# Scan constants in a PSUM bank, scans in two parts, turns in the channel mix's banks: a linear-attention and mixer kernel on one core

## The chip, the core and the metric

The kernel runs on one core of one Trainium2 chip. Its engines work side by side, each through its own list of instructions in order: TensorE (PE, with its weight loads as PEld), VectorE (DVE), ScalarE (ACT), GpSimd (POOL) and SyncE (SP), which issues the DMAs. The metric is the device time of one execution in microseconds, as the median of several runs; lower is better.

## The reference, cut to what matters

Four sequences of 768 steps go through a linear attention with a decay `w` per channel (8 heads of 48 channels), and its output `x` through a mixer: a low-rank mix over the steps (`U`, `V`, rank 32) and a channel mix (384 to 1536 to 384).

```python
for t in range(S):                                   # S = 768, state is [B, H, 48, 48]
    cur = einsum('bhd,bhe->bhde', u * k[t], v[t])
    y[:, :, t] = einsum('bhd,bhde->bhe', r[t], state + cur)
    state = w[t][..., None] * state + einsum('bhd,bhe->bhde', k[t], v[t])
...
h = x.transpose(0, 2, 1) @ U @ V
u = x + h.transpose(0, 2, 1)
return u + maximum(u @ w_ch1, 0.0) @ w_ch2
```

## The kernel before, in words

**Chunks.** Each sequence is cut into 6 chunks of 128 steps, so there are 24 chunks `g`. In a chunk the 8 heads lie as 4 pairs on 128 partitions, channels on partitions, steps along the free dimension. The running products of the decay come from two scans on DVE. `scan_f` (L387) runs backwards over `w` of all four pairs, 517 elements, with the constant `resets`, which is 1 at the border of a pair and 0 elsewhere, and so starts a new product in each pair. `tots` takes each pair's full product; a reciprocal (L423) puts its inverse into the border places of `qd`, which is 0 elsewhere, and `scan_q` (L400) runs forward over 516 elements with `qd`. Both constants lie in SBUF. Then `r` is multiplied with the result `Q` (step RP, L407) and `k` with `F` (step KS, L412), in place in the tile `rk`; each of these products runs on DVE or on GpSimd, as the order says. There is one buffer for `Q` and there are two for `F`.

**The rest of a chunk.** The scores (AM, into `aps`) are matmuls of the scaled `rk`. The diagonal, with the bonus `u`, comes from the products PR and MD in the first six chunks, and from RK, RU and a reduction RED on `kr` in the others; ACT or GpSimd lays it out as `A`; CP copies the scores above it under a mask (L557, L555). YA and YZ make `y`, DS the state's increment, ZA and ZM add and decay it. XE copies `y` into `xT`.

**Turns.** `k` (KT, copied out by ACT in L529) and `x` (XT, copied out in L743) are turned on PE for the first twelve chunks, later on DVE in blocks of 32. On PE these turns, and MD, write one PSUM bank of their own (`tr`, pool `psT`).

**Mixer.** When a sequence's six chunks are there, GA multiplies `x` with `U`: six chunk products of 32 rows and 384 columns, four beside each other, then two that add to the first two (L762). SELM and GSL (L782) make `gs` from it, HP (L816) the mix, UADD, UH and UL the two parts of `u`. The channel mix takes seven blocks of 384 or 512 steps. UP (L865) makes twelve groups of nine matmuls per block, each into one of three PSUM banks (`ffn`), which ACT and DVE empty (HH L870 or L872, HL L876). DN (L899) makes three sums per block, each in four quarters of nine matmuls, emptied by L917. The weights come as raw 64-bit words and are converted piece by piece (C2, C3 on DVE, E and HI on ACT, ADD on GpSimd, the remainder SUB, L339).

**What sets the order.** All steps stand in a list, and the table `ORDER` gives the sequence in which they are issued: three characters a step, its number, whether it goes to its other engine, and how many warming matmuls on constant data (`lead`, L200) go ahead of it. Each engine runs its steps in that sequence and waits by semaphores for what they need. Buffers and banks are handed out in the same sequence.

PSUM has eight banks: two for the scores, one each for the turns, `y` and the state, and three for the channel mix.

Of the kernel before, what the change touches and what calls it, by code (L numbers as in the profile page):

```python
# [20 lines left out]
P = 128  # L21
# [12 lines left out]
SEG = P + 1  # L34
# [17 lines left out]
def channel_order():  # L52
# [25 lines left out]
    "8I18w08y18x02505z08i02I02W02402O08l02K08m06A08n02109606W08o02L05+06G02608z02706X08j06a02c02218p09216Y19G06b0"
    "2802912X02Q09402Y02R02P09312M02N12S06e06f02d09s06H06K09702Z02j06c08u02T02U16L09J08k19L02l02e06g02a06h16d12k0"
    "6M08s02m09B09C09H06Z12f02g02n02q02b16N06l06O09506I02o16m09k06x09D06n02s09O19r09P02h06Q09M02r02i19E06y09Q02t0"  # L80
    "7106z06R07212u09j09K02p19l02v07302w17707806S0BB09F0Bc09N09R19t1BC09n09u19S19T09o09Y09806T0BE0BL09m17909W06U0"
    "6P09U19I09v09V16o09p16p09909X09q09Z09w19A16V0BJ06u06i06q0BR0Bb09a0BK0BG09y09b06J09x1BH0Be0C50BM06j06k09z0Bf1"
    "CY09d0BI1Bg06v06w09e0BN0Bj0BS07A0C806r07B0CF09f07D09+0Bl09c17C06s0Bh09-0Bk0CG1Bi1C916t07E0BV0BO0CH09g0BD0BP1"
    "6+0CA0740BT06-0BQ07F0BU0C607009h0CE0BW0D20Br0750A007G0760CX0A10Bm0CB0CI07H0Ch0D10BF1BZ0A30CD1A20Ca0A40BX0A50"
    "Bv0Bn0Ci1CC1Bo0CL0D407I0A60A70C707J07M0A807K07N07O0Bs0CJ1CK0A907P0Cc0BY1Bd0Cd0Cj0Cg0DT0Ck07S0Bt0AA0Bu0AD07Q0"
    "Dd0AE0AB0Ba07T0CM0AH0Bp0DB0Bq1AF0Bw07U0Bx0CP0AI0AJ0DA0Cf0B+0B-0DC1CN0Ga07V0AC0DU0By0Cn0Ce1CQ0D907W0AK0H40AG0"
    "AL0Gb0Bz17L0De0Gc0D60Co0CO0Ag0AM0AN0Am0D70CZ0An0Cb0GA0Ah0DW0AX0Ao0GQ0Cp0H50Ai0D81D50AU0AR0DD0AY0AZ0Cl1Db0Aa0"
    "C00AV07X0Dc0C10DY0GT07R0Cq0CR0DE0DZ0GR0CS0AW0Cr0Cm1CU0Da1Cs0DH0DV0CV0CT1Ad0Ct0Ab0G10Gd0CW0Cw0AS1AT0DI0Ac0DF1"
    "Cu0GB0C20Cx0Ae0D30GY0Af0DX1DL0AO0Cv1DG1G00DM0Df0Ap0Aj0Dg0DJ0AP0Dh0Cy0DQ0DR0Dj0AQ0DK0DN0Ge1G30Ak0Al0GC0As0Ha0"
# [1133 lines left out]
```

## Time and profile before

| | before |
|---|---|
| median of 3 runs | 450.12 us (448.71 to 450.27) |
| the profiled execution's own time | 448.02 us |
| its span on the core | 446.3 us |
| PE busy | 426.4 us (96%) |
| DVE busy | 362.7 us (81%) |
| ACT busy | 189.7 us (42%) |
| GpSimd busy | 104.0 us (23%) |

The span runs from the first instruction to the end of the last. Busy times are those of engine instructions; matmuls are pipelined and their ends modelled, so a busy PE may still wait a little between matmuls. The shares hide three stretches: up to the first up-projection at 68.3 us, from there to the last token-mix correction at 335.0 us, and the rest, in which only the channel mix is left.

### The profile page before, as it was taken

What the parts mean: (1) busy time and instruction counts of PE and PEld (TensorE: products, weight loads), DVE (VectorE), ACT (ScalarE), POOL (GpSimd) and SP (SyncE); (2) the same over time, 40 slices, a digit from 0 to 9 for tenths busy, and PEclk for the clock granted to TensorE, in tenths of its full rate; (3) what the DMA queues carried; (4) which work ended last, traced back from release to release, by engine and by line L of the source; (5) the groups of instructions that cost most, each with busy time, mean ns of one, the idle gap of its engine ahead of it and who ended that gap; (6) DMA issues with size and microseconds to landing.
All of it is one profiled execution on the core that took longest, in us unless ns stands there. A gap on an engine that the chain in (4) does not pass through costs nothing.

```text
span 446.3 us, 9868 instructions
## 1 busy us (share of the span) xinstructions
PE 426.4 (96%) x3906; PEld 366.1 (82%) x3906; DVE 362.7 (81%) x750; ACT 189.7 (42%) x533; POOL 104.0 (23%) x123
## 2 busy tenths in 40 slices
PE   6996999999999999999999999999999999999993
PEld 4785759999999898788868788887767889999993
DVE  8999999999899999999999999999995116524610
ACT  5697988776476332565023323013634002112300
POOL 1112232432257555332225101420000100100000
PEclk9996799999999999999999999999999999999998
DMA  8966836244654635331307030174212130133020
GB/s 298 337 232 225 271 124 220 87 153 151 223 171 164 220 106 181 107 115 37 107 32 241 3 93 0 46 225 164 74 66 77 36 122 21 59 127 110 1 78 24
DMA packets 23911, 57.22 MB, mean 128 GB/s; under 512 B 2864, under 2 KB 7856, under 8 KB 23856
## 3 DMA queue, kind: packets, MB, share of 16 engines
q1 hardware_dynamic: 23856, 56.50, 38.0%
q8 instruction: 32, 0.52, 0.5%
q14 instruction: 23, 0.19, 0.1%
HBM read 51.77 MB, written 4.72 MB: 127 GB/s over the span
## 4 chain that ended last, share of the span: by engine, by line
PE 40%; DVE 16%; issue 1%; ACT 1%; DVEq 0%
PE f L899 20%; PE f L865 16%; DVE xn L720 5%; DVE kn L685 2%; DVE hid L876 2%; DVE xn L718 1%; DVE A L555 1%; DVE F L387 1%; PE aps L542 1%; DVE Q L400 1%; PE hp L816 1%; DVE xT L917 1%; PE y L622 1%; DVE Z L593 0%; PE y L632 0%
## 5 line engine op out<-in xcount | busy, mean ns | idle before, releaser
L865 PE MATMUL f<-u,w1h 128*128 128x384 f32 (+1 forms) x504 | 147.9, 364 | 1.0 <-DVE hid L876 1.0
L899 PE MATMUL f<-hid,w2h 128*128 128x384 f32 (+1 forms) x504 | 148.3, 364 | 0.0
L865 PEld LDWEIGHTS f<-u,w1h 128*128 128x128 f32 x504 | 92.9, 188 | 12.6 <-DVE hid L876 2.5
L899 PEld LDWEIGHTS f<-hid,w2h 128*128 128x128 f32 x504 | 92.9, 188 | 10.0 <-issue 1.3
L865 PE MATMUL f<-u,w1l 128*128 128x384 f32 (+1 forms) x252 | 90.7, 360 | 0.0
L899 PE MATMUL f<-hid,w2l 128*128 128x384 f32 (+1 forms) x252 | 90.7, 360 | 0.0
L870 ACT ACTIVATE hid<-f 128x384 fp32r<-128x384 f32 (+1 forms) x65 | 34.6, 538 | 106.6 <-PE f L865 104.0
L876 DVE SCALAR_TENSOR_TENSOR hid<-f,hid 128x384 fp32r<-128x384 f32 (+1 forms) x84 | 50.2, 606 | 13.4 <-ACT hid L870 12.5
L454 ACT ACTIVATE A<-ident,dv 128x128 f32<-128x128 f32 x148 | 46.6, 391 | 11.7 <-DVE dv L440 3.9
L899 PEld LDWEIGHTS f<-hid,w2l 128*128 128x128 f32 x252 | 47.4, 188 | 4.7
L865 PEld LDWEIGHTS f<-u,w1l 128*128 128x128 f32 x252 | 47.4, 188 | 4.1
L685 DVE STREAM_TRANSPOSE kn<-rk 32x128 f32<-32x128 f32 x160 | 48.3, 302 | 2.4
L917 DVE TENSOR_TENSOR xT<-f,xT 128x384 f32<-128x384 f32 (+1 forms) x21 | 12.8, 613 | 37.6 <-PE f L899 37.2
L322 POOL TENSOR_TENSOR cva_w<-cva_w,raw_w 128x384 int32<-128x384 int32 x24 | 26.2, 1100 | 70.1 <-DVE cva_w L315 51.9
L832 POOL TENSOR_TENSOR u<-xT,u 128x512 fp32r<-128x512 f32 (+1 forms) x11 | 13.5, 1236 | 92.0 <-DVE u L828 85.1
L387 DVE TENSOR_TENSOR_SCAN F<-w,resets 128x517 f32<-128x517 f32 x24 | 30.6, 1275 | 0.4 <-DMA w<-in_wT 0.2
L720 DVE STREAM_TRANSPOSE xn<-xT 32x192 f32<-32x192 f32 x80 | 29.6, 370 | 1.3 <-ACT xT L666 0.2
L400 DVE TENSOR_TENSOR_SCAN Q<-w,qd 128x516 f32<-128x516 f32 x24 | 29.3, 1223 | 0.1
L407 POOL TENSOR_TENSOR rk<-rk,Q 128x512 f32<-128x512 f32 x12 | 16.4, 1365 | 45.0 <-DVE Q L400 42.3
L461 POOL TENSOR_SCALAR_AFFINE_SELECT A<-dv 128x128 f32<-128x128 f32 (+1 forms) x33 | 11.5, 382 | 58.1 <-PE f L865 23.3
L602 ACT ACTIVATE Z<-Z,tots 128x96 f32<-128x96 f32 x60 | 17.5, 364 | 10.3 <-DVE Z L593 10.2
L1088 ACT ACTIVATE junk<-raw_w 128x384 uint8<-128x384 f32 x24 | 13.1, 544 | 19.7 <-DMA raw_w<-in_w 19.5
(123 smaller groups left out, 570.8 us busy)
## 6 DMA issues: line engine op xcount, KB each, us to landing
raw_w<-in_w SPq DMA_DIRECT2D x48, 384.0 KB, 3.9
rk<-in_rkT SPq DMA_DIRECT2D x24, 512.0 KB, 4.3
kr<-in_rkN SPq DMA_DIRECT2D x18, 384.0 KB, 4.5
w<-in_wT SPq DMA_DIRECT2D x24, 258.5 KB, 2.8
v<-in_vS SPq DMA_DIRECT2D x24, 224.0 KB, 3.9
out_dram<-xT SPq DMA_DIRECT2D x12, 192.0 KB, 2.6
out_dram<-xT SPq DMA_DIRECT2D x9, 256.0 KB, 2.5
raw_V<-in_V SPq DMA_DIRECT2D x8, 96.0 KB, 3.4
```

The lines of the kernel that those rows point to most:

```text
L322: lambda: nc.gpsimd.tensor_tensor(out=d["to"].bitcast(I32), in0=d["a"].bitcast(I32), in1=d["e"], op=ALU.add),
L387: nc.vector.tensor_tensor_scan(out=F[:, ::-1], data0=st["w"][:, ::-1], data1=resets[:, ::-1], initial=1.0, op0=ALU.mult, op1=ALU.add)
L400: nc.vector.tensor_tensor_scan(out=st["Q"], data0=st["w"][:, 0:n], data1=qd, initial=0.0, op0=ALU.mult, op1=ALU.add)
L454: nc.scalar.activation(to, one, AF.Copy, scale=dv[:, NP * i + j : NP * i + j + 1])
L602: nc.scalar.activation(st["Z"][:, j], src[:, j], AF.Copy, scale=nxt[:, j : j + 1])
L685: nc.vector.transpose(a, b)
L720: nc.vector.transpose(to[q, :, :, r], src[r, :, :, q])
L865: nc.tensor.matmul(ps, wt[:, f, ct, :], u[ct][:, z], start=(m == 0), stop=(m == 8))
L870: nc.scalar.activation(h[:, 0], d["ps", f], AF.Relu)
L876: nc.vector.scalar_tensor_tensor(out=h[:, 1], in0=d["ps", f], scalar=0.0, in1=h[:, 0].bitcast(F32), op0=ALU.max, op1=ALU.subtract)
L899: nc.tensor.matmul(d["o", ct], wt[:, 4 * ct + part, f - 3 * part, :], hid[f][:, z], start=(part == 0 and m == 0), stop=(part == 3 and m == 8),
L917: nc.vector.tensor_tensor(out=o, in0=d["o", ct], in1=o, op=ALU.add)
```

## The change

- The two constants of the scans become one, `qd`, in a PSUM bank that nothing else uses (pool `psQ`). The turns' bank is given up for it. A bank holds 512 numbers, so a pair's stretch in `w`, `F` and `Q` becomes 130 long (`SEG`), and each scan runs as two instructions over two pairs each, 259 elements for F and 258 for Q; both halves read overlapping parts of `qd` (shifted by `OVER`). The inverses of the first and third pair go into a small tile `starts`, from which the Q scan takes its start value; those of the second and fourth go into `qd`. So the step R is two reciprocals.
- The turns of `k` and `x` and MD take one of the channel mix's three banks (`ffn`).
- In GA the products of the last two chunks of a sequence are each cut into two of 192 columns, so that four narrow ones stand beside each other and add to the four first sums.
- Small things: `blank`, 256 wide, takes the place of `resets` as data of the warming matmuls, and `w` in memory has the new stretch length.
- `ORDER` is a new table. Over the whole program it moves from DVE to GpSimd 5 products KS, 7 RP, 3 PR, 4 RK, 1 RU and 8 remainders SUB; five high parts HH go from DVE to ACT, three UH and two HI the other way; two decays ZM go from ACT to DVE.

```diff
-SEG = P + 1
+SEG = P + 2
+OVER = NP * SEG - NP * P
...
 ORDER = (
-    "2x03603002y03113203O03712z03303M03513P03V00J03803900L03400K03N03R03W13C03E23S02-03A10003D00200M00Q04e03B13X0"
+    "2x02y02z03M03N03000J03200003603712-03303803V03P03n03R03W13o00L03503903413Q10K03C03U03A14D03D03E03S03113T13X0"
...
-    psT = pool("psT", 1, space=PSUM)
     psY = pool("psY", 1, space=PSUM)
+    psQ = pool("psQ", 1, space=PSUM)
...
-    qd = const.tile([P, NP * SEG], F32, name="qd")
+    qd = psQ.tile([P, NP * P], F32, name="qd")
     nc.vector.memset(qd, 0.0)
+    nc.vector.memset(qd[:, SEG - 1 : NP * P : 2 * SEG - OVER], 1.0)
+    starts = const.tile([P, 2], F32, name="starts")
...
         def scan_f():
-            F = st["F"] = place("F", [P, NP * SEG + 1], f"F_{g}", buf["F"])
-            nc.vector.tensor_tensor_scan(
-                out=F[:, ::-1], data0=st["w"][:, ::-1], data1=resets[:, ::-1], initial=1.0, op0=ALU.mult, op1=ALU.add
-            )
+            F = st["F"] = place("F", [P, n], f"F_{g}", buf["F"])
+            for h in range(2):
+                a, e = 2 * SEG * h, 2 * SEG * (h + 1)
+                back = lambda t, o=0: t[:, a + 1 - o : e - o][:, ::-1]
+                nc.vector.tensor_tensor_scan(
+                    out=back(F), data0=back(st["w"]), data1=back(qd, OVER * h), initial=1.0, op0=ALU.mult, op1=ALU.add
+                )
...
         def scan_q():
             st["Q"] = place("Q", [P, n], f"Q_{g}", buf["Q"])
-            nc.vector.tensor_tensor_scan(
-                out=st["Q"], data0=st["w"][:, 0:n], data1=qd, initial=0.0, op0=ALU.mult, op1=ALU.add
-            )
+            for h in range(2):
+                a, e = 2 * SEG * h, 2 * SEG * (h + 1) - 2
+                nc.vector.tensor_tensor_scan(
+                    out=st["Q"][:, a:e], data0=st["w"][:, a:e], data1=qd[:, a - OVER * h : e - OVER * h],
+                    initial=starts[:, h : h + 1], op0=ALU.mult, op1=ALU.add,
+                )
...
-        rc = step(
-            "R " + nm, "DVE", lambda: nc.vector.reciprocal(qd[:, 0:n:SEG], st["F"][:, 1:n:SEG]), [f],
-            take=[buf["qd"]], use=[buf["F"]],
-        )
+        def invert():
+            tot = segs(st["F"])[:, :, 1]
+            nc.vector.reciprocal(starts, tot[:, 0:NP:2])
+            nc.vector.reciprocal(qd[:, SEG : NP * P : 2 * SEG - OVER], tot[:, 1:NP:2])
+
+        rc = step("R " + nm, "DVE", invert, [f], take=[buf["qd"]], use=[buf["F"]])
...
         def turn_k():
-            tr = st["trk"] = place("tr", [P, NP, P], f"trk_{g}", btr)
+            tr = st["trk"] = place("ffn", [P, NP, P], f"trk_{g}", btr)
...
-            for c in cs:
-                p0 = 32 * (c % 4)
+            n = 4 // len(cs)
+            for m in range(4):
+                c, w = cs[m // n], DM // n
+                cols = slice(m % n * w, m % n * w + w)
+                x = xns[b, c]["xn"].rearrange("p a b -> p (a b)")
                 nc.tensor.matmul(
-                    d["ga"][p0 : p0 + 32, :], U_sb[:, c, :], xns[b, c]["xn"], start=(c < 4), stop=(c >= NCH - 4)
+                    d["ga"][32 * m : 32 * m + 32, cols], U_sb[:, c, :], x[:, cols], start=(n == 1), stop=(n > 1)
                 )
```

What the new table does is seen best on the engines themselves. First DVE at the start of the program, before: the scans of the chunks 0 and 1 (`F`, `Q`), the pair product (`kr`), the products with `F` and `Q` (`rk`), the inverse (`RECIPROCAL`) and the first weight conversions (`cva`). A scan is listed here as SCALAR_TENSOR_TENSOR on L387 or L400 (L393 and L408 in the changed kernel).

```order
L387 SCALAR_TENSOR_TENSOR F_143<-w_140,resets 128x517
L423 RECIPROCAL qd<-F_143 128x4
L486 TENSOR_TENSOR kr_151<-rk_145 128x512
L400 SCALAR_TENSOR_TENSOR Q_154<-w_140,qd 128x516
L412 TENSOR_TENSOR rk_145<-rk_145,F_143 128x512
L387 SCALAR_TENSOR_TENSOR F_159<-w_156,resets 128x517
L302 TENSOR_SCALAR cva_w_1_171<-raw_w_1_162 128x384
L407 TENSOR_TENSOR rk_145<-rk_145,Q_154 128x512
L423 RECIPROCAL qd<-F_159 128x4
```

DVE at the same place, now:

```order
L393 SCALAR_TENSOR_TENSOR F_150<-w_141,qd 128x259 x2
L433 RECIPROCAL starts<-F_150 128x2
L434 RECIPROCAL qd<-F_150 128x2
L497 TENSOR_TENSOR kr_160<-rk_143 128x512
L408 SCALAR_TENSOR_TENSOR Q_164<-w_141,starts,qd 128x258 x2
L393 SCALAR_TENSOR_TENSOR F_173<-w_146,qd 128x259 x2
L433 RECIPROCAL starts<-F_173 128x2
L434 RECIPROCAL qd<-F_173 128x2
```

Each scan and each inverse is two instructions now, and the products of `rk` with `F` and `Q` are gone from here.

GpSimd's first products before are weight conversions alone:

```order
L322 TENSOR_TENSOR cva_w_1_171<-cva_w_1_171,raw_w_1_162 128x384
L322 TENSOR_TENSOR cva_V_300<-cva_V_300,raw_V_265 96x384
L322 TENSOR_TENSOR U_sb<-cva_U_207,raw_U_203 128x192
L322 TENSOR_TENSOR cva_w_2_326<-cva_w_2_326,raw_w_2_210 128x384
L322 TENSOR_TENSOR cva_w_0_482<-cva_w_0_482,raw_w_0_475 128x384
```

GpSimd's first products now:

```order
L421 TENSOR_TENSOR rk_143<-rk_143,F_150 128x512
L416 TENSOR_TENSOR rk_143<-rk_143,Q_164 128x512
L421 TENSOR_TENSOR rk_148<-rk_148,F_173 128x512
L416 TENSOR_TENSOR rk_148<-rk_148,Q_215 128x512
L324 TENSOR_TENSOR cva_w_1_184<-cva_w_1_184,raw_w_1_153 128x384
L497 TENSOR_TENSOR kr_243<-rk_182 128x512
L497 TENSOR_TENSOR kr_247<-rk_203 128x512
L341 TENSOR_TENSOR w1l<-cva_w_1_184,w1h 128x384
L416 TENSOR_TENSOR rk_182<-rk_182,Q_260 128x512
```

The products that left DVE stand here, ahead of the conversions and between them.

PE in the third chunk before: the turns of `k` (`trk`) and `x` (`trx`) share one bank, with other steps between them.

```order
L550 MATMUL aps<-rk_255 128x128 x8
L739 MATMUL trx_1_405<-ident,xT_275 128x128 x3
L564 MATMUL dS<-v_374,kn_324 48x48 x8
L520 MATMUL trk_421<-ident,rk_255 128x128 x4
L622 MATMUL y_452<-A_380,v_374 32x128 x8
```

PE there now:

```order
L561 MATMUL aps<-rk_182 128x128 x8
L575 MATMUL dS<-v_289,kn_308 48x48 x8
L503 MATMUL trd_392<-u_diag,kr_247 128x2 x4
L531 MATMUL trk_401<-ident,rk_182 128x128 x4
L531 MATMUL trk_408<-ident,rk_203 128x128 x4
L633 MATMUL y_433<-A_274,v_289 32x128 x8
```

MD (`trd`) and two turns of `k` stand side by side, in three of the channel mix's banks.

## Rows read from the trace of the kernel before

**Rows 1.** The page: busy us, share of the span and instructions of each engine.

```profile
PE 426.4 (96%) x3906; PEld 366.1 (82%) x3906; DVE 362.7 (81%) x750; ACT 189.7 (42%) x533; POOL 104.0 (23%) x123
```

**Rows 2.** Busy time of each engine by stretch; the first row names the columns.

```profile
core 0: us, PE busy (x) PEld busy (x) DVE busy (x) ACT busy (x) POOL busy (x), PEclk, DMA share, GB/s
0.00:68.30 68.30, 59.44 (x706) 44.81 (x707) 64.78 (x112) 53.00 (x158) 16.05 (x23) 0.90 0.72 244
...
26.00:36.00 10.00, 7.65 (x140) 6.03 (x133) 9.05 (x16) 8.86 (x28) 1.76 (x2) 1.00 0.64 222
36.00:50.00 14.00, 12.16 (x141) 9.64 (x142) 13.78 (x26) 11.19 (x33) 4.86 (x4) 0.51 0.80 265
...
68.30:333.70 265.40, 262.07 (x2645) 223.22 (x2644) 255.79 (x551) 117.80 (x323) 83.64 (x96) 1.00 0.38 124
333.70:446.30 112.60, 104.86 (x559) 98.03 (x558) 42.13 (x89) 18.88 (x55) 4.27 (x4) 0.98 0.20 68
```

**Rows 3.** Two lines' instructions: ns min/median/max, first and last start in us, forms.

```profile
L865 PE MATMUL f<-u,w1h x504: 332/336/505, 68.3 to 419.9; 128*128 128x384 f32 x96, 128*128 128x512 f32 x72
L782 DVE TENSOR_TENSOR gs<-gb,gs x4: 555/555/555, 63.7 to 335.0; 32x384 fp32r<-32x384 f32 x4
```

**Rows 4.** The chain that ended last, in order of time: start us, us, what.

```profile
253.87 2.08 PE f L865 x9
...
396.82 1.56 PE f L865 x9
```

**Rows 5.** The scans' and the inverse's lines, columns as in rows 3.

```profile
L387 DVE TENSOR_TENSOR_SCAN F<-w,resets x24: 1200/1226/2275, 3.6 to 292.4; 128x517 f32<-128x517 f32 x24
L400 DVE TENSOR_TENSOR_SCAN Q<-w,qd x24: 1211/1222/1233, 5.6 to 299.2; 128x516 f32<-128x516 f32 x24
L423 DVE RECIPROCAL qd<-F x24: 154/174/183, 4.9 to 295.1; 128x4 f32<-128x4 f32 x24
```

**Rows 6.** DVE: groups by form (busy us, mean ns), one line, a back-to-back pair.

```profile
L339 DVE TENSOR_TENSOR w1l<-cva_w,w1h 128x384 fp32r<-128x384 f32 x12 | 6.7, 555 | 0.1
L821 DVE TENSOR_TENSOR xT<-hp,xT 128x512 f32<-128x512 f32 x9 | 6.1, 683 | 0.5 <-PE hp L816 0.4
...
L407 DVE TENSOR_TENSOR rk<-rk,Q x12: 662/682/692, 8.7 to 268.7; 128x512 f32<-128x512 f32 x12
...
53.86 1.00 DVE L315 SCALAR_TENSOR_TENSOR cva_w<-raw_w,cva_w 128x384 uint32<-128x384 uint32 x2
L315 DVE SCALAR_TENSOR_TENSOR cva_w<-raw_w,cva_w 128x384 uint32<-128x384 uint32 x24 | 13.2, 556 | 0.1
```

**Rows 7.** Scans beside GpSimd's products: one line, then instructions by time (start, us).

```profile
L407 POOL TENSOR_TENSOR rk<-rk,Q x12: 1181/1202/2043, 84.0 to 300.5; 128x512 f32<-128x512 f32 x12
...
178.58 2.27 DVE L387 TENSOR_TENSOR_SCAN F<-w,resets 128x517 f32<-128x517 f32 x1
178.57 1.20 POOL L407 TENSOR_TENSOR rk<-rk,Q 128x512 f32<-128x512 f32 x1 [2.66 <-DVE tots L396]
...
133.15 1.21 DVE L387 TENSOR_TENSOR_SCAN F<-w,resets 128x517 f32<-128x517 f32 x1
133.31 2.04 POOL L407 TENSOR_TENSOR rk<-rk,Q 128x512 f32<-128x512 f32 x1 [2.61 <-DVE Q L400]
```

**Rows 8.** A product with one PSUM input on DVE, beside GpSimd, by time.

```profile
72.08 0.55 DVE L876 SCALAR_TENSOR_TENSOR hid<-f,hid 128x384 fp32r<-128x384 f32 x1
...
72.12 1.03 POOL L322 TENSOR_TENSOR cva_w<-cva_w,raw_w 128x384 int32<-128x384 int32 x1 [5.78 <-DVE cva_w L315]
```

**Rows 9.** PE by time: the sixteen score matmuls of two chunks.

```profile
17.32 2.08 PE L550 MATMUL aps<-rk 48*128 48x128 f32 x16
...
52.02 1.16 PE L550 MATMUL aps<-rk 48*128 48x128 f32 x16
```

**Rows 10.** PE by time: one batch's products of x and U.

```profile
149.19 1.46 PE L762 MATMUL ga<-xn,U_sb 128*32 128x384 f32 x12
```

**Rows 11.** ACT's copy of the turned k, columns as in rows 3.

```profile
L529 ACT ACTIVATE kn<-trk x10: 569/590/597, 10.1 to 128.2; 128x512 f32<-128x512 f32 x10
```

More of the change, by code (lines that the diff above doesn't have):

```diff
@@ L172, in rwkv_moe_kernel @@
     stage = pool("stage", 1)
-    slots = dict(big=BIG_BUFS, w=W_BUFS, v=2, F=2, Q=1, dv=2, kn=2, Z=2, tr=1, y=1, ffn=3, xT=3, xn=NCH // 2, cva=CVA_BUFS, g4=1, gs=2)
-    homes = dict(big=big, tr=psT, y=psY, ffn=psF, xT=xtp, cva=stage)
+    slots = dict(big=BIG_BUFS, w=W_BUFS, v=2, F=2, Q=1, dv=2, kn=2, Z=2, y=1, ffn=3, xT=3, xn=NCH // 2, cva=CVA_BUFS, g4=1, gs=2)
+    homes = dict(big=big, y=psY, ffn=psF, xT=xtp, cva=stage)
     turns = dict.fromkeys(slots, 0)
@@ L185, in place @@
         return homes.get(kind, sb2).tile(shape, dtype, tag=f"{kind}{n}", name=name)
-    resets = const.tile([P, NP * SEG + 1], F32, name="resets")
-    nc.vector.memset(resets, 0.0)
-    nc.vector.memset(resets[:, 0 : NP * SEG + 1 : SEG], 1.0)
+    blank = const.tile([P, 2 * P], F32, name="blank")
+    nc.vector.memset(blank, 0.0)
     ones = const.tile([P, 1], F32, name="ones")
-    nc.scalar.activation(ones, resets[:, 0:1], AF.Copy)
-    busy = resets.bitcast(BF16)[:, 0:512]
+    nc.vector.memset(ones, 1.0)
+    busy = blank.bitcast(BF16)
     idle = place("ffn", [P, 512], "idle")
@@ L358, in load_w @@
         def load_w():
-            st["w"] = place("w", [P, NP * SEG + 1], f"w_{g}", buf["w"])
+            st["w"] = place("w", [P, NP * SEG], f"w_{g}", buf["w"])
             nc.sync.dma_start(st["w"], wT[b, c])
@@ L481, in chunk @@
         if by_pe:
-            btd = Buf("tr")
+            btd = Buf("ffn")
             def prod(eng):
@@ L488, in rows_by_u @@
             def rows_by_u():
-                tr = st["trd"] = place("tr", [P, NP, P], f"trd_{g}", btd)
+                tr = st["trd"] = place("ffn", [P, NP, P], f"trd_{g}", btd)
                 lead(tr)
@@ L732, in turn @@
             return
-        btr = Buf("tr")
+        btr = Buf("ffn")
         def go():
-            tr = d["tr"] = place("tr", [P, NP, P], f"trx_{b}_{c}", btr)
+            tr = d["tr"] = place("ffn", [P, NP, P], f"trx_{b}_{c}", btr)
             lead(tr)
@@ L948, in recurrence @@
                 st, vt = (full("xT", f"{n}_{j}") for n in ("st", "vt"))
-                nc.sync.dma_start(chunks(wt), wb[:, :, j * SEG + 1 : (j + 1) * SEG])
+                nc.sync.dma_start(chunks(wt), wb[:, :, j * SEG + 1 : j * SEG + 1 + P])
                 nc.sync.dma_start(chunks(rt), rb[:, 0, j])
@@ L955, in recurrence @@
                     nc.sync.dma_start(vn, vb4[:, c, j])
-                    tr = place("tr", [P, NP, P], f"trv_{j}_{c}")
+                    tr = place("ffn", [P, NP, P], f"trv_{j}_{c}")
                     nc.tensor.transpose(tr[0:VW, 0, :], vn, ident)
```

95 lines of the change are left out of this document (49 added, 46 removed).

## The prediction

> **What bounds the kernel now.** The first view is the table of busy times by stage, because the page's shares [rows 1] are means over three stages with different limits. I cut the span at two points: the first up-projection starts at 68.3 us, and the last correction of the token mix (the low part of `gs`, the fourth of four) at 335.0 us [rows 3]. Before 68.3 us no channel mix exists, and DVE is busy 64.78 of 68.3 us, 95% [rows 2]. From 68.3 to 333.7 us PE is busy 262.07 and DVE 255.79 of 265.4 us: both nearly full. After that PE alone works on the channel mix that is left [rows 2], group after group without a gap: nine matmuls of 512 columns take 2.08 us, nine of 384 take 1.56 us [rows 4]. The reader should see that PE has a fixed amount of channel mix, that it can begin it only when DVE has brought six chunks through, and that it hardly pauses from then on. So the time is the start of the first up-projection plus what PE and DVE need after it. A microsecond taken from DVE ahead of 68.3 us is worth nearly a microsecond; one taken from it between 68.3 and 333.7 us is worth something only as far as PE can follow; after that, nothing.
>
> **Part 1, the scans in two parts, as DVE time.** A Q scan over 516 elements takes 1.222 us, an F scan 1.226 us, an inverse 0.174 us [rows 5]. What a half takes isn't in the trace. Two lengths of a plain product, 384 and 512 columns at 0.555 and 0.682 us [rows 6], give about 0.99 ns per element and 0.17 us of fixed time. With that fixed time a scan costs (1.222 - 0.17) / 516 = 2.04 ns per element, and a half of 258 costs 0.70 us: two halves are 0.17 us dearer than one scan. Back to back, two instructions of 0.556 us take 1.00 us together [rows 6], 0.11 less than their sum, and the second half doesn't wait for the first; by that spacing the split costs 0.06 us. The second inverse costs 0.17 us by its own length, 0.06 by spacing. Reading the constant from PSUM: a product with one PSUM operand of 512 columns takes 0.683 us against 0.682 from SBUF alone [rows 6], so I add nothing. The start value of the Q scan now comes from memory; no row shows that. Between zero and another shortest instruction (0.17 us) I take zero, since the operand is two numbers.
>
> The Trainium skill (Perfetto Trace Analysis, Optimizing Scalar/DVE Operations) puts the fixed cost of a DVE instruction at about 60 ns on SBUF and 125 ns on PSUM, a rule against this change: 65 ns on each of 96 halves would be an estimated 6.2 us, and the forecast below would become 448 us. The two products [rows 6] don't show this difference.
>
> **Part 2, what leaves DVE.** The constants in SBUF made each scan an instruction with two SBUF inputs, and such an instruction and a GpSimd product exclude each other. At 178.58 us an F scan that starts 0.01 us after a GpSimd product takes 2.27 us in place of 1.23; at 133.31 us a product that starts during a scan takes 2.04 us in place of 1.20 [rows 7]. A DVE instruction with one input in PSUM and a GpSimd product run beside each other at 0.55 and 1.03 us, their usual times [rows 8]. So the new scans should leave GpSimd free, and the new order uses that: it gives GpSimd 28 more products in all.
>
> Counted in the order up to the last low part of block 0's `u`, DVE has 104 steps before and 85 now. Gone are 7 products by Q, 2 by F, 3 pair products (512 columns, 0.68 us: 8.2 us), 5 products of the row form and 3 weight remainders (384 columns, 0.55 us: 4.4 us), and one reduction (0.5 us): 13.1 us. Added are one more F scan (1.4 us) and one decay of the state (0.5 us): 1.9. The splits cost 16 x 0.17 = 2.7 us and 8 x 0.17 = 1.4 us. Net 7.1 us less by lengths; by spacing, with 0.11 off each moved instruction too, 13.1 - 2.2 - 1.8 - 1.4 = 7.7. GpSimd gets 18 more steps there, about 20 us at 1.20 us [rows 7] and less for the short ones, and is busy 16.05 of 68.3 us now [rows 2]; it has the room. Where it is late, DVE is held: there is one Q buffer, so a Q scan waits until GpSimd has read the last one, and the copy with the mask, the next chunk's scans and the weight conversions queue behind it. Between two Q scans DVE mostly has 2.7 us of other work, against one product of 1.20 us and what stands ahead of it.
>
> PE is what comes up next. It is busy 59.44 of those 68.3 us [rows 2], and its clock isn't always full: 0.51 is granted from 36 to 50 us [rows 2], and sixteen score matmuls take 2.08 us at 17.3 us against 1.16 at 52.0 us [rows 9], the lower level early on as well. PE had idled just before the clock fell (7.65 us busy from 26 to 36 [rows 2]). The order has 29 warming matmuls in place of 20 ahead of the first up-projection. I take 6 of the 7 to 8 us: the first up-projection at about 62 us.
>
> **Part 3, from there to 333.7 us.** DVE loses 3 products of 512 and 5 remainders of 384, one F scan, two high parts (now ACT's), one low part and one total: 7.9 us. It gains two casts of `u`, two of weights, one decay and one reduction: 2.5 us. Splits: 31 x 0.17 + 16 x 0.17 = 8.0 us by lengths, 2.8 by spacing. Net between 2.6 us more and 2.6 us less on an engine with 9.6 idle us there [rows 2]; I take zero. As many up groups (26) and down quarters (34) stand behind the last correction in both orders, so the tail of 112.6 us stays.
>
> **Part 4, the narrow products.** The twelve token-mix matmuls of a batch take 1.46 us in four sets [rows 10], some 0.33 us a set. Two sets become half as wide: 0.33 us less per batch, three times behind the first up-projection. 1.0 us.
>
> **Part 5, the turns.** They lose their own bank and use the channel mix's three. In the start this helps, as two turns can be open. Eight of them stand behind the first up-projection; each bank is free again after ACT's copy, 0.59 us [rows 11]. I cost them at nothing: a group takes 1.56 us [rows 4], which covers matmuls and copy while ACT is prompt. If that cover is gone, see the rivals. The shorter memsets at the start: 0.2 us, left out.
>
> **The sum.** 448.02 us was the profiled execution's own time; less 6.0 and 1.0 gives 441.0. The median of the runs was 450.12, 2.1 above it; I put the median at 1 us above, 442.0 us.
>
> **Rivals.** *PE at the lower clock paces the start.* For it: busy 59.44 of 68.3 us, nine more warming matmuls. Against: fewer pauses may keep the clock up. If the first up-projection comes only 1 us earlier, with the narrow products: 448 us, no change. Chance 0.16.
>
> *The halves are dearer.* The place is DVE up to 333.7 us, 96 halves and 24 inverses. At 0.07 us more a half the 7 us are gone; slower by my measure begins at about 0.11 us. At the bound of 0.17 us (the start value costs one more short instruction): 16 us, 458 us. Against: the equal products [rows 6]. No change 0.05, slower 0.03.
>
> *Turns hold PE up.* If ACT is late, each of the eight turns costs PE one group, 8 x 1.56 = 12.5 us: 454.5 us, slower. It decides from about 1.3 us a turn. For it: ACT is busy 53.0 of 68.3 us at first [rows 2], and a high part queued behind other copies frees its bank late. Against: DVE and ACT take turns at emptying banks, and PE has three. Chance 0.09.
>
> *The change doesn't do what it says:* the scans still exclude GpSimd's products. The 28 moved products then meet scans, and a meeting costs 0.84 to 1.05 us [rows 7]; half of them, 13 us: 455 us, slower. Against: [rows 8]. Chance 0.05.
>
> *A scan runs faster with one operand in PSUM,* at the product's 0.99 ns per element: 2 x 0.43 = 0.86 us for 1.22. DVE gets 17 us back, but PE binds soon: some 4 us more in the start, 1 behind it, 437 us. Against: products with both inputs in SBUF already run at 0.99 ns [rows 6], so the second SBUF read isn't what slows the scan. Chance 0.05.
>
> **Chances.** The forecast, 442 us (437 to 447), has 0.57. Within 0.5% of 450.12, about what a measurement of this kernel can tell from no change, lies 447.9 to 452.4. Faster: 0.57 + 0.05 = 0.62. Same: 0.16 + 0.05 = 0.21. Slower: 0.03 + 0.09 + 0.05 = 0.17. The range goes down to 434.5: DVE's full 7.7 us in the start, the middle 2.6 us lighter and the narrow products give 448.0 - 11.3 = 436.7 with nothing put on top, and 2 us are for half of the faster scans. It goes up to 452.0, which takes in no change and leaves out the slower cases.
>
> **What would show it.** The first up-projection at 62 us (58 to 66); halves of 0.70 us (0.65 to 0.75) with none near 1.5 us; GpSimd products beside scans at 1.20 us; DVE busy still about 95% up to the last correction, which comes near 328 us; a tail of 112 us. A first up-projection at 67 us with PE full means the clock; gaps on PE ahead of up groups behind a turn's copy mean the banks; halves of 0.8 us and more mean Part 1 was wrong.

## The result and the profile after

The changed kernel takes **442.43 us** (median of four runs, 442.31 to 442.92) against 449.41 us before on the same chip: a ratio of 0.9855, interval 0.9813 to 0.9897, so 1.5% faster. A second series gave 442.17 us against 447.91: 0.9871 (0.9837 to 0.9906), 1.3% faster. The profiled execution of the first series took 442.49 us.

The page of the changed kernel, its span and its busy times, answers [rows 1]:

```profile
span 440.8 us, 10001 instructions
PE 422.5 (96%) x3931; PEld 364.3 (83%) x3931; DVE 349.9 (79%) x796; ACT 184.4 (42%) x517; POOL 131.7 (30%) x157
```

The same three stages as in [rows 2], with the cuts at the first up-projection and at the start of the last correction. Columns are the stretch, its length, then busy time (and instructions) of PE, PEld, DVE, ACT, POOL, then granted clock, DMA share and GB/s. The second block is the middle of the kernel before, cut in the same way:

```profile
0.00:62.56 62.56, 56.17 (x723) 43.51 (x723) 57.23 (x119) 49.74 (x149) 34.85 (x40) 0.81 0.80 269
62.56:329.10 266.54, 262.80 (x2657) 223.65 (x2656) 253.35 (x593) 118.05 (x324) 93.61 (x114) 1.00 0.42 130
329.10:440.80 111.70, 103.53 (x555) 97.16 (x553) 39.34 (x86) 16.65 (x46) 3.20 (x3) 0.99 0.16 51
```

```profile
68.31:335.00 266.69, 263.36 (x2650) 224.08 (x2649) 256.71 (x553) 118.38 (x324) 83.64 (x96) 1.00 0.38 125
```

The cuts come from the two lines that answer [rows 3] (ns min/median/max, first and last start in us):

```profile
L879 PEld LDWEIGHTS f<-u,w1h x504: 186/188/191, 62.6 to 413.8; 128*128 128x128 f32 x168
L796 DVE TENSOR_TENSOR gs<-gb,gs x4: 555/555/555, 58.0 to 329.1; 32x384 fp32r<-32x384 f32 x4
```

Of the 5.5 us between the two profiled executions the start gives 5.7: the first up-projection moves from 68.3 to 62.6 us. From there to the last correction it was 266.7 us and is 266.5; the tail was 111.3 us and is 111.7. In the start DVE does 57.23 us of work instead of 64.78, GpSimd 34.85 instead of 16.05. The scans, the inverses and GpSimd's products with them, against [rows 5] and [rows 7]:

```profile
L393 DVE TENSOR_TENSOR_SCAN F<-w,qd x48: 657/670/694, 3.6 to 279.0; 128x259 f32<-128x259 f32 x48
L408 DVE TENSOR_TENSOR_SCAN Q<-w,starts,qd x48: 712/729/751, 5.8 to 299.8; 128x258 f32<-128x258 f32 x48
L433 DVE RECIPROCAL starts<-F x24: 146/158/168, 4.9 to 282.7; 128x2 f32<-128x2 f32 x24
L434 DVE RECIPROCAL qd<-F x24: 145/153/163, 5.0 to 282.7; 128x2 f32<-128x2 f32 x24
L416 POOL TENSOR_TENSOR rk<-rk,Q x19: 1182/1197/1414, 7.3 to 300.7; 128x512 f32<-128x512 f32 x19
L421 POOL TENSOR_TENSOR rk<-rk,F x15: 1176/1192/1241, 6.1 to 245.4; 128x512 f32<-128x512 f32 x15
```

The longest scan of before took 2.27 us, the longest half now 0.75. The chain of waits shows what paces the end of the start now (start, us, what; most pieces left out):

```profile
34.04 2.34 PE y L200 x9
...
42.41 1.14 PE trx L200 x7
43.55 0.33 PE trx L750 x3
43.87 0.97 PE trk L200 x6
...
50.81 0.65 PE y L200 x3
...
57.75 0.65 PE y L200 x4
...
62.63 0.37 PE f L879
```

From 34 us on this chain is PE's, with short pieces of ACT, and 5.75 us of it are the warming matmuls (L200).

### The profile page after: what moved, and what is told of

Its sections match the earlier page's. It is cut to its first block, busy times and chain, and to the rows that moved or that the text cites. A ratio compares the mean times of both kernels' runs of the same rounds, so it can differ in the third digit from the quotient of the medians.

```text
span 440.8 us, 10001 instructions
## 1 busy us (share of the span) xinstructions
PE 422.5 (96%) x3931; PEld 364.3 (83%) x3931; DVE 349.9 (79%) x796; ACT 184.4 (42%) x517; POOL 131.7 (30%) x157
## 4 chain that ended last, share of the span: by engine, by line
PE 51%; DVE 37%; issue 4%; ACT 3%; DMA 2%; SPq 0%; DVEq 0%; ACTq 0%
PE f L913 19%; PE f L879 19%; DVE kn L696 8%; DVE xn L731 6%; DVE hid L890 4%; DVE Q L408 3%; DVE A L566 3%; DVE F L393 3%; PE aps L561 2%; PE y L633 2%; DVE xn L729 1%; DVE xT L835 1%; ACT A L465 1%; DMA w<-in_wT 1%; PE y L643 1%
## 5 line engine op out<-in xcount | busy, mean ns | idle before, releaser
L884 ACT ACTIVATE hid<-f 128x384 fp32r<-128x384 f32 (+1 forms) x70 | 37.2, 541 | 142.5 <-PE f L879 97.7
L465 ACT ACTIVATE A<-ident,dv 128x128 f32<-128x128 f32 x140 | 43.9, 393 | 4.9 <-DVE dv L451 4.8
L416 POOL TENSOR_TENSOR rk<-rk,Q 128x512 f32<-128x512 f32 x19 | 23.5, 1236 | 46.9 <-DVE Q L408 33.0
L408 DVE TENSOR_TENSOR_SCAN Q<-w,starts,qd 128x258 f32<-128x258 f32 x48 | 33.2, 733 | 0.2
L393 DVE TENSOR_TENSOR_SCAN F<-w,qd 128x259 f32<-128x259 f32 x48 | 30.4, 675 | 1.8 <-DMA w<-in_wT 1.6
L421 POOL TENSOR_TENSOR rk<-rk,F 128x512 f32<-128x512 f32 x15 | 17.9, 1196 | 15.5 <-DVE F L393 8.2
L886 DVE TENSOR_SCALAR hid<-f 128x384 fp32r<-128x384 f32 (+1 forms) x14 | 8.2, 584 | 15.9 <-PE f L879 15.9
```

Of the source, the lines that this page charges most:

```text
L393: nc.vector.tensor_tensor_scan(out=back(F), data0=back(st["w"]), data1=back(qd, OVER * h), initial=1.0, op0=ALU.mult, op1=ALU.add)
L408: nc.vector.tensor_tensor_scan(out=st["Q"][:, a:e], data0=st["w"][:, a:e], data1=qd[:, a - OVER * h : e - OVER * h], initial=starts[:, h : ...
L416: ENG[eng].tensor_tensor(out=rk[:, 0], in0=rk[:, 0], in1=Qv, op=ALU.mult)
L421: ENG[eng].tensor_tensor(out=rk[:, 1], in0=rk[:, 1], in1=F5, op=ALU.mult)
L465: nc.scalar.activation(to, one, AF.Copy, scale=dv[:, NP * i + j : NP * i + j + 1])
L884: nc.scalar.activation(h[:, 0], d["ps", f], AF.Relu)
```

## The experiments

All runs, cut at the same two events. The kernel before had medians of 447.8 to 448.0 us beside these runs.

| run | median us | start ends | middle | tail |
|---|---|---|---|---|
| before | 449.41 | 68.3 | 266.7 | 111.3 |
| changed kernel | 442.43 | 62.6 | 266.5 | 111.7 |
| the same, second series | 442.17 | 62.8 | 266.6 | 111.7 |
| constant in SBUF | 471.24 | 74.5 | 283.3 | 111.8 |
| products back on DVE | 460.11 | 68.8 | 277.2 | 111.7 |
| products back in the start only | 448.38 | 69.2 | 265.8 | 111.8 |
| more DVE work in the middle | 448.41 | 63.3 | 271.7 | 111.7 |
| halves in the old arrangement | 455.63 | 70.2 | 272.2 | 111.3 |
| wide products with U | 443.64 | 65.6 | 269.1 | 111.7 |
| start value a number | 442.00 | 60.5 | 265.2 | 111.7 |
| no warming matmuls | 441.37 | 63.5 | 265.8 | 111.6 |
| first nine warming matmuls only | 440.58 | 61.1 | 265.8 | 111.6 |
| the same again | 440.23 | 61.9 | 266.0 | 111.6 |
| the same, diagonals on GpSimd | 443.25 | 61.9 | 265.8 | 111.8 |

The stages are those of one profiled execution each. That of the wide products (448.15 us) is the slowest of its eight times and that of the last row (441.20 us) the fastest, so their stages don't stand for their medians.

**The constant in SBUF.** The theory: the constant in PSUM is what lets GpSimd run beside the scans. The rival: order and engine choice alone make the gain.

```diff
-    psQ = pool("psQ", 1, space=PSUM)
...
-    qd = psQ.tile([P, NP * P], F32, name="qd")
+    qd = const.tile([P, NP * P], F32, name="qd")
```

> The changed kernel with one edit: the constant operand of both scans lies in SBUF again; the bank that held it stays empty, and halves, order and turns are as changed. Theory A (the constant in PSUM is what lets GpSimd run beside the scans): the half scans that meet a GpSimd product grow from 0.67-0.75 to 1 us or more, GpSimd's products L416 and L421 climb from a median of 1.20 to as much as 2 us, the first up-projection starts 2 to 6 us later than at 62.6, and the time is 445 to 450 us. Theory B (the earlier start comes from order and engine choice alone): the scans lengthen by at most 0.05 us on average and the time stays at 442 to 443.5 us.

It takes 471.24 us, 28.8 more than the changed kernel: the direction of theory A, but more than 20 us above its range, with a start 11.9 us later where 2 to 6 were expected. One place with the same instructions in both traces shows the mechanism: the changed kernel first, then this one, two Q halves on DVE and a product on GpSimd that starts 0.16 to 0.17 us behind the first (start, us):

```profile
245.25 1.37 DVE L408 TENSOR_TENSOR_SCAN Q<-w,starts,qd 128x258 f32<-128x258 f32 x2
245.42 1.18 POOL L421 TENSOR_TENSOR rk<-rk,F 128x512 f32<-128x512 f32 x1 [7.81 <-DVE F L393]
```

```profile
272.25 2.26 DVE L407 TENSOR_TENSOR_SCAN Q<-w,starts,qd 128x258 f32<-128x258 f32 x2
272.41 1.54 POOL L420 TENSOR_TENSOR rk<-rk,F 128x512 f32<-128x512 f32 x1 [8.24 <-DVE F L392]
```

With the constant in SBUF product and halves hold each other up; with it in PSUM all three take their usual time. The groups and the stages of this kernel:

```profile
L407 DVE TENSOR_TENSOR_SCAN Q<-w,starts,qd 128x258 f32<-128x258 f32 x48 | 47.4, 1028 | 0.2
L392 DVE TENSOR_TENSOR_SCAN F<-w,qd 128x259 f32<-128x259 f32 x48 | 47.4, 1027 | 0.5 <-DMA w<-in_wT 0.4
0.00:74.50 74.50, 58.41 (x723) 45.17 (x723) 72.65 (x119) 50.10 (x149) 41.42 (x40) 0.77 0.67 230
74.50:357.80 283.30, 268.43 (x2657) 225.46 (x2656) 270.42 (x593) 118.25 (x324) 105.07 (x114) 0.99 0.37 122
```

The scans together take 94.8 us instead of 63.6 (33.2 and 30.4 on the changed kernel's page). That is 31.2 us on DVE, and the time grows by 28.8. The rival falls: with the constant in SBUF the same order and engine choices are 5.2% slower than the kernel before. The Trainium skill (SBUF — State Buffer, Who interferes with whom) says that a DVE instruction with two SBUF inputs contends with a GpSimd instruction that reads SBUF, and one with at most one such input, outside its two-port modes, doesn't; the two pairs of rows agree. What surprised is the middle: it grows by 16.8 us for 17.1 us of added DVE time, though DVE seemed to have 13 idle us there.

**The products back on DVE.** In all 44 steps whose engine the change had altered among KS, PR, RP, RK, RU and SUB, the old engine, in the new order; one line of the table shows the form (the third character of a step holds its engine, odd for the other one, and twice the number of its warming matmuls):

```diff
-    "3B13Y00M03b00N03q00O03r13x04C04M03s03F03G03t04F04H01404e03Z10Q03d03O03a13e08P01503w00P03H10103u13c03v13y04d0"
+    "3B13Y00M03b00N03q00O03r13x14C04M13s03F03G03t04F04H01404e03Z10Q03d03O03a13e08P01503w00P13H10103u03c03v13y04d0"
```

> The changed kernel with the products of KS, PR, RP, RK, RU and SUB on the engines that they had before (44 change engine, net 28 return to VectorE); order, halves, banks otherwise as changed. Theory A (what was gained is VectorE work moved to GpSimd in the start): the first up-projection starts near 68 us instead of 62.6, the middle stays at 266-268 us, the time is 446 to 450 us. Theory B (by 34 us into the start TensorE with its warming matmuls is the pacer, so that VectorE has slack there): only 1 to 3 us of it come back and the time is 443 to 446 us.

460.11 us, outside both. The start did what the first theory said (68.8 us), the middle didn't (277.2 us). Its stages, and a wait of DVE between 115 and 150 us (us in total, times, longest):

```profile
0.00:68.80 68.80, 55.95 (x723) 42.95 (x723) 66.89 (x136) 50.23 (x149) 16.34 (x23) 0.83 0.74 249
68.80:346.00 277.20, 266.73 (x2658) 225.24 (x2656) 259.67 (x603) 118.50 (x324) 82.83 (x103) 0.99 0.38 124
DVE kr L444 <- DMA kr<-in_rkN: 4.0, 1, 4.0
```

The middle has 6.3 us more on DVE, and DVE waits 4.0 us there for one load; together 10.3 of the 10.7 us that it grows. Why the load is late isn't shown. Two runs separate start and middle.

**The products back in the start only.** The same for the 19 steps that stand ahead of the first up-projection, among them the weight remainder SUB of `V` and the product RP 6, which this line of the table shows:

```diff
-    "7d04v07e00A07y04905G13l00b03L00p01C04W00c04AE7-04sC0B01D04t04Y00q00e04Z04X10f00d11E07f10g04a05H04f05I03m01F0"
+    "7d04v07e00A07y04905G13l00b03L00p01C04W00c04AE7-04sC0B11D04t04Y00q00e04Z04X10f00d11E07f00g04a05H04f05I03m01F0"
```

> The changed kernel with 19 engine choices of the start alone as before (18 products return to VectorE, one goes to GpSimd, net some 11.5 us of VectorE work); the middle keeps its choices. Theory A (the whole gain is VectorE work moved to GpSimd in the start, and the middle keeps its own pace): the first up-projection starts at 67.5 to 70 us, as in the run with all products back (68.8), the middle takes 266 to 268.5 us, the time is 447.5 to 451 us. Theory B (a start that is busier on VectorE also leaves the middle short of converted weights or of finished chunks): the middle takes 270 us or more and the time is 452 us or more.

448.38 us, ratio to before 1.0009 (0.9986 to 1.0032). The whole gain is gone, all of it in the start:

```profile
0.00:69.20 69.20, 59.87 (x724) 46.17 (x724) 67.13 (x136) 50.11 (x149) 16.34 (x23) 1.00 0.74 247
69.20:335.00 265.80, 262.30 (x2657) 223.52 (x2655) 252.61 (x592) 117.80 (x324) 93.83 (x114) 1.00 0.40 130
```

Theory A holds (its middle came out 0.2 us under the range), and a later start by itself leaves the middle as it is. The 29 warming matmuls are in this kernel too, so they alone don't make the gain.

**More DVE work in the middle.** A copy that nobody needs; the edit puts it behind the two Q halves of chunks 10 to 17, not behind the inverses as the expectation says:

```diff
+            if 10 <= g < 18:
+                nc.vector.tensor_copy(spare, qd)
```

> The changed kernel with one added VectorE copy of 128x512 (a new tile that nobody reads) after the reciprocal step of chunks 10 to 17, eight in all, some 0.65 us each, 5.3 us; the result is as before. Theory A (in the middle TensorE sets the pace and VectorE, idle 13 of 266.5 us, hides some of it): 0 to 2 us more, 442 to 444.5 us. Theory B (both engines are equally late there, so that work added to VectorE counts in full although work taken from it gives nothing): 4 to 5.5 us more, 446.5 to 448 us.

```profile
L414 DVE COPY spare<-qd x8: 658/666/672, 104.6 to 201.0; 128x512 f32<-128x512 f32 x8
63.30:335.00 271.70, 263.93 (x2657) 223.22 (x2656) 259.74 (x601) 117.74 (x324) 93.95 (x114) 1.00 0.39 128
DVE hid L893 <- ACT hid L887: 2.9, 4, 1.4
```

Eight copies, 5.3 us; the middle 5.1 us longer than in the second series, the time 6.2, 0.4 above theory B's range. Theory B. In the longer middle DVE is still idle 12.0 us, so idle time gave these copies little room. About half of it, 6.3 us, is nine waits for ACT and PE (us, times, longest; the largest group is shown); the other half is some 300 gaps of under 0.15 us. In the changed kernel's own profile nine waits come to 7.4 us, 1.1 more. The copies stand between 104 and 201 us; the middle's other parts weren't loaded.

**Halves in the old arrangement.** The old table, the turns in a bank of their own, the constant in SBUF; of the change only the halves and the narrow products with U stay. Against the changed kernel, without the table and the lines that name the turns' bank:

```diff
+    psT = pool("psT", 1, space=PSUM)
...
-    psQ = pool("psQ", 1, space=PSUM)
...
-    qd = psQ.tile([P, NP * P], F32, name="qd")
+    qd = const.tile([P, NP * P], F32, name="qd")
```

> The kernel before (its order and engine choices, turns in a bank of their own, constant in SBUF) with only the halved scans and the narrow products with U. Halves measure 0.67 and 0.73 us where nothing collides, against 1.23 for a whole scan: some 0.17 us more per pair of halves and 0.3 us for the second start value, 48 scans, some 12 us of VectorE in all, 4 of it in the start. Theory A (VectorE's work counts in full in the start and nearly so in the middle): 6 to 12 us slower than the kernel before, 454 to 461 us. Theory B (halves let GpSimd in between, the lock waits shrink, and the middle hides the rest): within 3 us of the kernel before, 446 to 452 us.

```profile
L393 DVE TENSOR_TENSOR_SCAN F<-w,qd x48: 660/678/1731, 3.7 to 300.5; 128x259 f32<-128x259 f32 x48
0.00:70.20 70.20, 60.69 (x711) 45.68 (x711) 66.94 (x137) 52.66 (x158) 15.68 (x23) 0.76 0.70 238
70.20:342.40 272.20, 265.21 (x2662) 224.69 (x2660) 264.14 (x600) 118.24 (x324) 82.53 (x96) 0.99 0.37 122
```

455.63 us, 1.0157 of before (1.0107 to 1.0208), as theory A said: the split, with the narrow products, costs 7.7 us here. The order and the free GpSimd have to earn that first. A half with the constant in SBUF takes 0.678 us in the median, from PSUM 0.670: reading this operand from PSUM costs a scan nothing that these rows show. The old order with the constant in PSUM wasn't tried: it has the turns open in such a sequence that they need a bank of their own or a fourth `ffn` bank, and there is none. So order and banks aren't separated.

**Wide products with U.** GA as before, six products of 384 columns:

```diff
-            n = 4 // len(cs)
-            for m in range(4):
-                c, w = cs[m // n], DM // n
+            for c in cs:
+                p0 = 32 * (c % 4)
```

> The changed kernel with the products of x and U in their old form: six of 384 columns instead of eight of 192 per sequence and half. Theory A (the narrow form saves TensorE 0.33 us in each of three sequences that it has to spare nowhere else): 0.5 to 1 us slower than the changed kernel, 442.7 to 443.5 us. Theory B (the 1.0 us of the forecast goes into gaps that TensorE has anyway before the last chunks are done): within 0.3 us of the changed kernel, 441.9 to 442.6 us.

443.64 us (eight times, 442.65 to 448.15) against 442.17 and 442.43: theory A's side, 0.1 above its range. By the medians the narrow form is worth 1.2 to 1.5 us. The two kernels were not run side by side, and the ratios to the kernel before (0.9898, 0.9862 to 0.9935, against 0.9871, 0.9837 to 0.9906) overlap, so the size is uncertain.

**The start value a number.** The column of inverses as start value of the Q halves is replaced:

```diff
-                    initial=starts[:, h : h + 1], op0=ALU.mult, op1=ALU.add,
+                    initial=0.0, op0=ALU.mult, op1=ALU.add,
```

> The changed kernel with the number 0 as start value of both Q half scans instead of the column of inverses; the first element of each half loses its start value, so what is left out is the inverse total in the Q scans. Theory A (the start value read from a tile is what makes a Q half 0.06 us dearer than an F half): the Q halves fall from 0.73 to 0.67 us, 2.9 us less VectorE work in all, and since VectorE's work in the start gives its time back the time is 441 to 442 us. Theory B (the difference lies in the data or the length): Q halves stay at 0.73 us, the time at 442.2 us.

```profile
L408 DVE TENSOR_TENSOR_SCAN Q<-w,qd x48: 652/669/694, 5.7 to 296.6; 128x258 f32<-128x258 f32 x48
```

Theory A on the price: 0.06 us for reading the start value. On the time nothing is shown: 439.15 us in the profiled execution, but 441.63 to 442.91 in the other four.

**No warming matmuls ahead of the turns.** All counts in the table to zero; in the run after this one all but the first nine. Two of the four lines:

```diff
-    "4k10X04504T03k047I5807Z07z07b00G05D04q14V04U04r17j05A10Z04800H00I14614u00905E08705903K07k10n00a01B05F10o00Y0"
-    "7d04v07e00A07y04905G13l00b03L00p01C04W00c04AE7-04sC0B01D04t04Y00q00e04Z04X10f00d11E07f10g04a05H04f05I03m01F0"
...
+    "4k10X04504T03k04705807Z07z07b00G05D04q14V04U04r17j05A10Z04800H00I14614u00905E08705903K07k10n00a01B05F10o00Y0"
+    "7d04v07e00A07y04905G13l00b03L00p01C04W00c04A07-04s00B01D04t04Y00q00e04Z04X10f00d11E07f10g04a05H04f05I03m01F0"
```

> The changed kernel without any warming matmul ahead of the turns (29 of them left out, which take 5.75 us of the chain of waits between 34 and 62 us). Theory A (they keep the granted clock at full speed and are worth their time): without them the clock stays at half speed for 10 us or more of the stretch from 34 us to the first up-projection, which starts later than 62.6 us, and the time is 443 to 450 us. Theory B (they are only in the way): the first up-projection starts at 58 to 61 us and the time is 438 to 441 us.

441.37 us, between the theories. The score matmuls show why: sixteen of them around 41 us, in the changed kernel and in this one (start, us):

```profile
40.44 1.16 PE L561 MATMUL aps<-rk 48*128 48x128 f32 x16
```

```profile
41.00 2.08 PE L561 MATMUL aps<-rk 48*128 48x128 f32 x16
...
48.52 1.16 PE L561 MATMUL aps<-rk 48*128 48x128 f32 x16
```

Without warming the clock is still at its lower level at 41 us and full by 48.5. What the 5.75 us of warming give back and what the slower matmuls take nearly cancel. (The granted clock reads 1.00 for this whole start, because the trace's records of it begin only at 47.8 us, as they begin at 40.1 us in the run with the products back in the start; the matmuls' own times tell.)

**The first nine only.** They stand at 34 us, ahead of the rise; the other 20 come when the clock is full.

```diff
-    "7d04v07e00A07y04905G13l00b03L00p01C04W00c04AE7-04sC0B01D04t04Y00q00e04Z04X10f00d11E07f10g04a05H04f05I03m01F0"
+    "7d04v07e00A07y04905G13l00b03L00p01C04W00c04A07-04s00B01D04t04Y00q00e04Z04X10f00d11E07f10g04a05H04f05I03m01F0"
...
-    "5P00i07a07n17q05Q08201005R07r00+07o00j08315S08O05T00t01100w01W08Y07u87p07v08R05U05Y01I05c05V00k07s05Z05W05a0"
+    "5P00i07a07n17q05Q08201005R07r00+07o00j08315S08O05T00t01100w01W08Y07u07p07v08R05U05Y01I05c05V00k07s05Z05W05a0"
```

> The changed kernel with only the first group of nine warming matmuls (at 34.0 us, where the clock is at half speed); the other 20, worth 3.4 us of the chain of waits between 42 and 59 us, are left out. Theory A (TensorE paces the end of the start and the clock, once full at 38.2 us, stays full without them): the first up-projection starts at 59.5 to 61.5 us, the time is 439 to 441 us. Theory B (the clock falls again in the gaps, or VectorE takes over as pacer at once): the start stays within 1 us of 62.6 or is later, and the time is 442 to 446 us.

440.58 us, with the first up-projection at 61.1 us: theory A. Once more:

> The kernel that kept only the first nine warming matmuls once more, unedited. If the 440.58 us of its first four times was its own, 440 to 441.5 us here too, below every time of the changed kernel in its two series (441.9 to 442.9 us). If it was the spread of the start, the times overlap that band, with a median of 441.5 to 443 us.

```profile
40.53 1.16 PE L561 MATMUL aps<-rk 48*128 48x128 f32 x16
0.00:61.10 61.10, 54.35 (x703) 42.15 (x703) 56.94 (x119) 49.62 (x149) 34.78 (x40) 0.97 0.82 276
```

440.23 us, 0.9817 of before (0.9778 to 0.9856); all six times lie below the changed kernel's. (The two lines are from the first of these two series.) Ten times lie at 439.12 to 441.96, the changed kernel's eight at 441.9 to 442.9. The clock is full at 40.5 us as with all 29, and 3.4 us of warming are gone from PE's chain; 1.6 to 2.2 of them arrive in the median. This version beats both kernels by its times; set against the kernel before in its own series it gains 1.5 and 1.8%, the changed kernel 1.5 and 1.3%, and those intervals overlap.

**Diagonals on GpSimd.** Five diagonal steps of the start from ACT to GpSimd, in the version with nine warming matmuls; one line of four:

```diff
-    "4G14n03g03h14j03i00C00l00W15504104O00604P11A14404E04S04Q15C10704o02+04l10D04p00E05B05700m07Y03j04h15610F0080"
+    "4G14n03g03h14j03i00C00l00W15504104O00604P01A14404E04S04Q05C10704o02+04l10D04p00E05B05700m07Y03j04h15610F0080"
```

> The kernel that kept only the first nine warming matmuls (440.58 us), with five of the diagonal-building steps of the start (of chunks 3, 5 and 6) moved from ACT, where four of 0.30 us follow each other, to GpSimd, which is idle from 29.6 to 32.9, 37.0 to 41.4 and 49.5 to 53.5 us there. Theory A (with the warming matmuls gone, ACT paces the end of the start): the first up-projection starts at 59 to 60.5 us instead of 61.1, the time is 438.5 to 440 us. Theory B (the GpSimd steps come late, or VectorE is next at once): the start stays at 61 us or later, the time is 440 to 442 us.

```profile
L482 POOL TENSOR_SCALAR_AFFINE_SELECT A<-dv x5: 630/634/2957, 27.4 to 49.4; 128x512 f32<-128x512 f32 x5
0.00:61.90 61.90, 53.81 (x703) 41.53 (x703) 59.02 (x119) 44.19 (x129) 40.46 (x45) 0.89 0.80 274
38.39 3.54 POOL L482 TENSOR_SCALAR_AFFINE_SELECT A<-dv 128x512 f32<-128x512 f32 x2 [1.52 <-ACT dv L508]
39.83 1.03 DVE L317 SCALAR_TENSOR_TENSOR cva_w<-raw_w,cva_w 128x384 uint32<-128x384 uint32 x2
```

443.25 us: above the range of theory B too, with the start at 61.9 us as B said. ACT loses 5 us of work, but GpSimd and DVE meet again: one diagonal step takes 2.96 us beside a run of DVE products, and the same 119 DVE instructions take 59.02 us instead of 56.94. That this is what makes the median 2.7 to 3.0 us longer isn't shown: the profiled execution is the fastest of its series, and its stages are those of the version without the move.

## Why the prediction was right

**The start.** The step "6 of the 7 to 8 us" held: 62 us forecast, 62.6 and 62.8 measured. DVE's net of 7.1 to 7.7 us was 7.55, and the products back in the start alone undo the gain. Of the 7.55 us 5.75 came through, 76%, where the text took 6 of 7 to 8; DVE is idle 5.3 us in the start, 3.5 before. The longest waits in it (us, times, longest) are for the score matmuls and for a load:

```profile
DVE A L568 <- PE aps L561: 1.8, 3, 0.7
DVE F L393 <- DMA w<-in_wT: 1.6, 3, 0.8
```

So PE did come up next, as the text said, and the loads with it.

**The halves.** 0.70 us was the mean of what came: 0.670 for F, 0.729 for Q. That the mean is so close is luck in part, as F came out 0.03 us cheaper and Q 0.03 dearer. The step "I take zero" for the start value was 0.06 us short; with the number in its place a Q half falls to F's length. PSUM at no extra cost held (0.670 against 0.678 us). The Trainium skill's higher fixed cost for PSUM (Perfetto Trace Analysis, Optimizing Scalar/DVE Operations) isn't borne out by these two rows. The second inverse added 0.14 us (0.158 and 0.153 for 0.174), 0.17 was taken. GpSimd's 20 us were 18.8.

**The middle.** Its forecast of no change held, its reason only on one side. DVE's work there fell from 256.71 to 253.35 us, 3.4 us less, where the forecast had 2.6 more to 2.6 less; the stretch became 0.2 us shorter. The words "an engine with 9.6 idle us there" read as slack, and the added copies showed that between 104 and 201 us there is hardly any: 5.3 us of DVE work put in made the stretch 5.1 us longer. Work taken from it isn't shown to give time: neither these 3.4 us did, nor the 2.9 us less in the Q scans, with which the median didn't move. PE can't follow far, being busy 262.8 of 266.5 us.

**The narrow products.** The 1.0 us was about right as a price (1.2 to 1.5 by the medians), and PE's own rows bear it out: in the middle the products with U took 4.82 us before and take 3.90 (stretch, length, PE, PEld, clock, DMA share, GB/s; before, then now).

```profile
68.31:335.00 266.69, 4.82 (x36) 1.16 (x36) 1.00 0.38 125
62.56:329.10 266.54, 3.90 (x48) 1.21 (x48) 1.00 0.42 130
```

Yet middle and tail together didn't become shorter in the changed kernel. In the same stretch its 967 channel-mix matmuls took 208.40 us instead of 207.28 (their ends are modelled), and PE was idle 3.7 us instead of 3.3. The turns in the channel mix's banks, costed at nothing, are the nearest suspect, but the trace speaks against them: the last turn on PE starts at 142.9 us, and from the first up-projection to 146 us PE waits for more than 0.15 us only once (us, times, longest):

```profile
PE f L879 <- DVE hid L890: 0.2, 1, 0.2
```

In the runs that differ only in the start (products back, no warming, the first nine twice) the middle took 265.8 to 266.0 us, 0.7 to 0.9 us less than before, so that most of the gain shows there. Why the changed kernel's own profiles have 266.5 and 266.6 us stays open.

**The sum.** The profiled execution was forecast at 441.0 us and took 442.49: the 1.0 us of the narrow products, 0.3 of the start and 0.2 behind it were missing. The median, put 1 us above, came at 442.43, level with its profile. So it is luck that the median came within 0.5 us: the addition for the spread made up for the missing gain. The 450.12 us from which the spread was taken was itself high, as the later medians of the kernel before are 447.8 to 448.0 us. The range's lower end, 436.7 less 2, is 434.7 and not 434.5 us; nothing hangs on it.

**The rivals.** Scans that still exclude GpSimd's products: refuted by the pair of rows, and the run with the constant in SBUF shows that the rival was priced too low, 13 us for what would have been 28.8. Dearer halves: the Q halves are 0.03 us dearer than 0.70, the F halves 0.03 cheaper, far from 0.07 more on each. A faster scan from PSUM: no. The turns: no loss near 12.5 us. PE at the lower clock: in the run without warming it does pace the stretch from 34 to 48 us. With the 5.75 us of warming saved, the first up-projection comes 0.9 us later than in the changed kernel (63.5 against 62.6 us), and 1.6 to 2.4 us later than with the first nine warming matmuls alone; the other 20, 3.4 us, cost more than they give. The clock isn't what made the gain: without warming most of it stays (441.37 us), and with all 29 but the products back on DVE it is gone (448.38 us).

## What to carry to other kernels

An operand that moves to PSUM can be worth far more through what it lets another engine do than through its own instruction: price the collision, not the operand. Idle time isn't slack by itself: here half of it was short gaps between instructions and half a few waits, and added work filled little of either. So before calling a stage hidden, put a known amount of work into it and see how much comes out. Warming matmuls paid here ahead of the clock's rise; look on the chain of waits whether the later ones stand in the way.

## What the runs showed of the hardware

- With its constant in SBUF a scan and a GpSimd product hold each other up (two Q halves 2.26 us, the product 1.54); with the constant in PSUM they don't (1.37 and 1.18).
- A scan whose start value is read from a tile takes 0.729 us for 258 elements, with a number 0.669.
- A GpSimd instruction can be held up through a run of DVE instructions, not only through one: the diagonal step of 2.96 us (usually 0.63) began at 38.4 us, while DVE ran products and weight steps that followed each other without a gap until 40.9.
- The clock rose earlier with nine warming matmuls at 34 us than without (full by 40.5 us against some time between 43.1 and 48.5), and 20 more after the rise changed nothing about it.
